# Unit 0's feed-forward by pairs of blocks, attention bundles half a step sooner, late key products further back: one kernel on one Trainium2 core

## The chip, the cores and the metric

The kernel runs on one core of a Trainium2 chip. The metric is the device time of one execution in microseconds (us), as the median of several runs. A core has five engines that run side by side, each through its own list of instructions in order: PE (TensorE, matrix products), DVE (VectorE, element by element), ACT (ScalarE, functions and copies), POOL and SP, which here issues nearly all the DMAs. PE multiplies from SBUF into PSUM, which has eight banks; DVE and ACT read PSUM and write SBUF. An instruction that waits holds up everything behind it on its engine.

## The reference, cut to what matters

```python
# q, k, v, a_re, a_im: (4, 8, 768, 48)
mag = sqrt(a_re**2 + a_im**2)
scale = minimum(mag, 0.999) / (mag + 1e-06)
a_re_n, a_im_n = a_re * scale, a_im * scale
for t in range(768):                       # S_re, S_im start at zero
    S_re, S_im = ar * S_re - ai * S_im + kv, ar * S_im + ai * S_re
    y[:, :, t] = einsum('bhd,bhde->bhe', q[:, :, t], S_re)
x = y, heads side by side                  # (3072, 384)
out = ((x @ w_a) * (x @ w_b)) @ w_out      # 384 -> 1536 -> 384
```

A linear recurrence with complex decay gives x, and a gated feed-forward net follows. All data are float32.

## The kernel before, in words

**Units.** Tokens are worked in chunks of 128 (six per sequence) and two of the four batch rows at a time. So there are 12 units: units 0 to 5 are the chunks of the first two rows, 6 to 11 those of the last two. Units 5 and 11 are the last chunks and pass no state on.

**Stages of a unit u.**
- `prep(u)` (L204 to L343) normalizes the decay, forms its running products and multiplies q and k with them. It is DVE work with some functions on ACT. Late in it: squares (ACT, L302), their sum (DVE, L308), logarithm and exponential (ACT, L309, L310), two products (DVE, L328, L330), the key product (DVE, L334) and the products of q and k (DVE, L314). The next unit's normalization, `scale` (L171), is woven in (ACT L182 to L191, DVE L183 to L197).
- `stack(u)` (L348) moves q and k from the tile qk to the tile stk by ten SBUF to SBUF DMAs on SP. There is one qk and one stk: stk is written once the attention ahead has read it, and `load_qk` (L345) of the next unit once the stacking has read qk.
- `attn(u)` (L377), for each batch row i of the two and each group of four heads: scores (PE L391) and their mask (DVE L394, the tile am), transposes of k (PE L402, copied by ACT L406), outputs (PE L431, bank x), their cast to xh (ACT L435) and the rest xl (DVE L440), and the new state (PE L447, DVE L454 and L458).
- The feed-forward of unit w works in 12 blocks of 128 columns. First products (`gemm1`, PE L498): 18 matmuls a block, on xh and xl, into banks called ab. `gated` multiplies: a copy on ACT (L502), the product h_t on DVE (L503), its cast hh on ACT (L504), the rest hl on DVE (L505). Second products (`gemm2`, PE L534): 6 matmuls a block. From unit 1 on two blocks make a pair: one bank takes a of both blocks and one b of both, so each step of `gated` works on 512 columns. The first bank is free for the next pair after L502, the second after L503.

**Start.** The weights come as 64-bit numbers and are split into two float32 parts (`split_weights`, L135) on DVE, PE and ACT, a part of it during unit 0's feed-forward. There unit 0 goes block by block (256 columns in `gated`), over three ab banks and two m banks, which scores, transposes and states share; after that there are two and three.

**Order.** While the feed-forward of unit w runs, the attention of unit w+1 is called in bundles, between the pairs. A step k counts blocks. At even k a pair's first products are called, at odd k the second products of the pair before; a bundle follows step k where k stands in `SLOTS` (L59) or, for units 5 and 11, `SLOTS_LAST`. The last bundle also ends prep(w+2) and calls its stacking, then load_qk(w+3). `drain` (L648) lets prep advance between steps by about 2400 ns of work, as its `yield`s count it. A scheduler then orders each engine's instructions by priority (the masks, casts and gated steps are raised). From w = 4 on (`LED`) PE keeps the order as written.

Of the kernel before, what the change touches and what calls it, by code (L numbers as in the profile page):

```python
# [46 lines left out]
EARLY = 2  # L47
WARM = 8
LED = 5
O_BUFS = 3  # L50
# [7 lines left out]
STACK_AT = 11  # L58
SLOTS = ((5, 7, 9, 11), (5, 7, 9, 11), (5, 7, 9, 10))  # L59
SLOTS_LAST = (6, 8, 10)  # L60

# [10 lines left out]
def tile_kernel(ctx: ExitStack, tc: tile.TileContext, a_d, qk_d, v_d, w_d, qn_d, kn_d, vn_d, an_d, out_d):  # L72
# [12 lines left out]
    ps = fast.enter_context(tc.tile_pool(name="ps", bufs=1, space=PSUM))  # L85
    turns = {"ab": [0, 1, 2], "o": [3, 4], "x": [5], "m": [6, 7]}

# [116 lines left out]
    def prep(u):  # L204
# [120 lines left out]
        if u < EARLY:  # L325
# [5 lines left out]
                                 op0=ALU.subtract, op1=ALU.mult, reverse0=True)  # L331
        yield 870
        kk = qk[:, :, 1, TOK:2 * TOK]
        vec.tensor_tensor(out=kk, in0=kk, in1=a_t[:, 0].rearrange("p (j t) -> p j t", j=NJ), op=ALU.mult)  # L334
        if rescaled(c):
# [9 lines left out]
    def load_qk(u):  # L345
        sync.dma_start(out=qk[:, :, 1, 0:2 * TOK], in_=qk_d[u])
# [30 lines left out]
    def attn(u, xh, xl):  # L377
# [82 lines left out]
        if u == 0:  # L460
            order = [(scores, 0, 0), (scores, 0, 1), (outputs, 0, 0), (outputs, 0, 1), (scores, 1, 0), (scores, 1, 1),
                     (residual, 0, 0), (outputs, 1, 0), (outputs, 1, 1), (transposes, 0, 0), (transposes, 0, 1),
                     (residual, 1, 0), (state, 0, 0), (transposes, 1, 0), (transposes, 1, 1), (state, 1, 0)]
        elif u == 1:
            order = [(scores, 0, 0), (scores, 0, 1), None, (transposes, 0, 0), (transposes, 0, 1), None,
                     (outputs, 0, 0), (outputs, 0, 1), (scores, 1, 0), (scores, 1, 1), (residual, 0, 0), None,
                     (state, 0, 0), None, (transposes, 1, 0), (transposes, 1, 1), None,
                     (outputs, 1, 0), (outputs, 1, 1), (residual, 1, 0), (state, 1, 0), None]
        elif last:
            order = [(scores, 0, 0), (scores, 0, 1), None,  # L470
                     (outputs, 0, 0), (outputs, 0, 1), (residual, 0, 0), (scores, 1, 0), (scores, 1, 1), None,
                     (outputs, 1, 0), (outputs, 1, 1), (residual, 1, 0), None]
        else:
            order = [(scores, 0, 0), (scores, 0, 1), (transposes, 0, 0), None,
                     (transposes, 0, 1), (outputs, 0, 0), (outputs, 0, 1), (residual, 0, 0), (scores, 1, 0), None,
                     (scores, 1, 1), (state, 0, 0), (transposes, 1, 0), None,
                     (transposes, 1, 1), (outputs, 1, 0), (outputs, 1, 1), (residual, 1, 0), (state, 1, 0), None]
# [205 lines left out]
    for w in range(NU):  # L683
# [6 lines left out]
        if w + 1 == LED:  # L690
            ordered.enter_context(tc.manual_schedule(engines={pe.engine}))
        if w == 0:
            for f in range(NF):
                next(ws, None)
                drain(p1, P1_F)
                if f == P1_AT:
                    drain(p1)
# [6 lines left out]
                    pgen = prep(2)  # L704
                pend.extend((w, os_, *h) for h in gemm1((f,), *x_cur))
                if len(pend) > LAG:
                    second()
                if f > STACK_AT - 6:
                    next(at, None)
            turns["ab"], turns["m"] = [0, 1], [2, 6, 7]  # L710
            drain(at)
            drain(pgen)
            stack(2)
            load_qk(3)
            pgen = prep(3)
            x_cur = x_nxt
            continue
        slots = () if last else SLOTS_LAST if (w + 1) % NCH + 1 == NCH else SLOTS[min(w, len(SLOTS)) - 1]
        for k in range(NF):
            if last and k >= NF - 2:  # L720
# [7 lines left out]
            if k in slots:  # L728
                next(at)
                if k == slots[-1]:  # L730
# [4 lines left out]
                    if w + 3 < NU:  # L735
                        load_qk(w + 3)
                        pgen = prep(w + 3)
            drain(pgen, 2400)
        x_cur = x_nxt
# [70 lines left out]
```

## Time and profile before

| | us |
|---|---|
| median of 3 runs | 694.71 (694.18 to 695.41) |
| the profiled execution, its own time | 697.03 |
| its span, first to last instruction | 694.9 |
| PE busy | 647.5 |
| DVE busy | 542.4 |
| ACT busy | 290.2 |
| granted PE clock, mean | 0.969 |

Busy times are of the whole span. The page also cuts the span into 40 slices, with each engine's busy share in tenths. A timeline row has the start in us, the duration, the engine, the line, the operation, the tiles it writes and reads, the matrix or tile sizes, a count, and in brackets how long the engine had stood idle before it and what it waited for. A row of a group has the count, busy us and mean ns, then the idle time before its instructions.

### The profile page before, as it was taken

Reading aid. Unit: us, or ns where it says so; the run is one execution under the profiler, and the core shown is the slowest. Engines: PE = TensorE matmul, PEld = TensorE weight load, DVE = VectorE, ACT = ScalarE, POOL = GpSimd, SP = SyncE. Lnnn points to the kernel's source line nnn. Section 1 sums busy time; section 2 is a strip of 40 time slices with the busy share of each in tenths; the row PEclk is TensorE's granted clock in tenths of the full one; section 3 lists DMA queues with packets and bytes.
Section 4 is the critical chain, followed back from the end, with each engine's and each line's share of the span. In section 5 each row is a group of like instructions: output and inputs, shape, how many; then the busy total and the mean of one; then the engine's idle time right before and its main releaser. Section 6 shows DMA issues by size and latency. Waiting matters only on the chain.

```text
span 694.9 us, 14053 instructions
## 1 busy us (share of the span) xinstructions
PE 647.5 (93%) x5854; PEld 609.0 (88%) x5854; DVE 542.4 (78%) x1081; ACT 290.2 (42%) x484; POOL 5.6 (1%) x11
## 2 busy tenths in 40 slices
PE   2647999999999999999899999999999989999996
PEld 1224889898999999999799999999899989999996
DVE  5999999999889999999888989989899542213211
ACT  6357665624445255362444634445241412121211
POOL 3000000000000000000000000000000000000000
PEclk9577999999999999999999999999999999999999
DMA  8973201413315133160430521430420420400000
GB/s 312 403 285 106 90 1 38 147 55 88 110 38 148 51 115 107 23 208 7 118 119 20 150 69 46 116 113 9 122 70 1 122 69 2 121 24 2 24 1 27
DMA packets 32085, 63.91 MB, mean 92 GB/s; under 512 B 3984, under 2 KB 10640, under 8 KB 32016
## 3 DMA queue, kind: packets, MB, share of 16 engines
q1 hardware_dynamic: 28560, 58.23, 27.2%
q10 hardware_dynamic: 3456, 4.72, 1.9%
q8 instruction: 48, 0.79, 0.5%
q14 instruction: 21, 0.17, 0.1%
HBM read 39.32 MB, written 4.72 MB: 63 GB/s over the span
## 4 chain that ended last, share of the span: by engine, by line
PE 55%; DVE 32%; DMA 5%; ACT 3%; issue 3%; SPq 1%; ACTq 0%; DVEq 0%
PE ab L498 28%; PE o L534 13%; PE pm L391 4%; PE xp L431 4%; DVE a_t L294 3%; PE pm L447 3%; DVE qk L314 2%; DMA w<-in_dram 2%; DVE h_t L503 2%; DVE hl L505 2%; DVE pr L231 2%; DVE z L299 2%; DVE pr L261 2%; PE pm L402 1%; DVE o_sb L143 1%
## 5 line engine op out<-in xcount | busy, mean ns | idle before, releaser
L498 PE MATMUL ab<-xh,w 128*128 128x256 f32 x1728 | 325.8, 283 | 5.0 <-ACT xh L435 2.7
L498 PEld LDWEIGHTS ab<-xh,w 128*128 128x128 f32 x1728 | 272.2, 189 | 6.8 <-ACT xh L435 3.3
L498 PE MATMUL ab<-xl,w 128*128 128x256 f32 x864 | 243.8, 282 | 1.7 <-DVE xl L440 1.7
L498 PEld LDWEIGHTS ab<-xl,w 128*128 128x128 f32 x864 | 163.8, 190 | 3.1 <-DVE xl L440 2.7
L534 PE MATMUL o<-w,hh 128*128 128x384 f32 x576 | 149.9, 340 | 0.0
L503 DVE TENSOR_TENSOR h_t<-ab,h_t 128x512 f32<-128x512 f32 (+1 forms) x79 | 50.5, 639 | 76.6 <-PE ab L498 71.5
L504 ACT CAST hh<-h_t 128x512 fp32r<-128x512 f32 (+1 forms) x79 | 45.8, 580 | 135.8 <-DVE h_t L503 135.7
L534 PEld LDWEIGHTS o<-w,hh 128*128 128x128 f32 x576 | 100.0, 188 | 0.8 <-issue 0.6
L534 PE MATMUL o<-w,hl 128*128 128x384 f32 x288 | 97.1, 337 | 0.0
L502 ACT COPY h_t<-ab 128x512 f32<-128x512 f32 (+1 forms) x79 | 42.9, 544 | 110.6 <-PE ab L498 98.5
L505 DVE TENSOR_TENSOR hl<-h_t,hh 128x512 fp32r<-128x512 f32 (+1 forms) x79 | 50.6, 641 | 12.6 <-ACT hh L504 12.4
L151 PE MATMUL ab<-o_sb,ident 128*128 128x384 f32 x42 | 27.9, 770 | 30.4 <-DVE o_sb L145 20.6
L391 PE MATMUL pm<-stk 128*128 128x128 f32 x384 | 52.9, 280 | 1.9 <-DMA stk<-qk 1.9
L534 PEld LDWEIGHTS o<-w,hl 128*128 128x128 f32 x288 | 54.0, 188 | 0.0
L391 PEld LDWEIGHTS pm<-stk 128*128 128x128 f32 x384 | 48.2, 191 | 6.1 <-issue 2.8
L231 DVE TENSOR_TENSOR pr<-z 128x384 f32<-128x384 f32 (+1 forms) x91 | 47.2, 525 | 2.8 <-ACT z L217 0.6
L294 DVE TENSOR_TENSOR a_t<-z,b_t 128x768 f32<-128x768 f32 x48 | 44.3, 953 | 0.1
L151 PEld LDWEIGHTS ab<-o_sb,ident 128*128 128x128 f32 x42 | 9.8, 277 | 39.2 <-DVE o_sb L145 29.0
L314 DVE TENSOR_TENSOR qk<-qk,z 128x768 f32<-128x768 f32 (+1 forms) x34 | 43.7, 1286 | 0.5
L431 PE MATMUL xp<-am,v_t 128*32 128x128 f32 x768 | 39.1, 276 | 0.6 <-DVE am L394 0.6
L394 DVE TENSOR_TENSOR am<-pm,mask 128x512 f32<-128x512 f32 x48 | 32.5, 684 | 3.5 <-PE pm L391 3.2
L431 PE MATMUL xp<-stk,u 128*32 128x128 f32 x640 | 32.9, 273 | 0.0
(105 smaller groups left out, 749.2 us busy)
## 6 DMA issues: line engine op xcount, KB each, us to landing
w<-in_dram SPq DMA_DIRECT2D x36, 384.0 KB, 8.1
qk<-in_dram SPq DMA_DIRECT2D x12, 768.0 KB, 4.8
a_t<-in_dram SPq DMA_DIRECT2D x11, 768.0 KB, 4.4
stk<-qk SPq DMA_DIRECT2D x42, 192.0 KB, 3.3
v_t<-in_dram SPq DMA_DIRECT2D x24, 256.0 KB, 2.7
out_dram<-o_sb ACTq DMA_DIRECT2D x24, 192.0 KB, 2.0
stk<-qk SPq DMA_DIRECT2D x18, 192.8 KB, 3.2
stk<-qk SPq DMA_DIRECT2D x14, 128.0 KB, 2.7
```

The lines of the kernel that those rows point to most:

```text
L151: pe.matmul(out=lp[:, 0:n], lhsT=ident, rhs=t, start=True, stop=False)
L231: vec.tensor_tensor(out=pr[:, :, :, o:o + n], in0=view(zz, W + at_(i) + 2 * o, [[W, 2], [-W, 2], [2, n]]), in1=tok(slice(1, 3), i - 1, o, ...
L294: vec.tensor_tensor(out=pz[:, s].rearrange("p (j b e) -> p j b e", j=SUB // 2, e=2), in0=zb[:, 1 + s], in1=view(bb, (1 + k - s) * NB, [[0, ...
L314: vec.tensor_tensor(out=qk4[:, :, k, x0:x1], in0=qk4[:, :, 1, x0:x1], in1=z[:, k].rearrange("p (j t) -> p j t", j=NJ).unsqueeze(2).broadca ...
L391: pe.matmul(out=sp[:, h4], lhsT=stk[:, h, ks], rhs=stk[:, h, qs], start=True, stop=True)
L431: pe.matmul(out=xp[qd * 32:(qd + 1) * 32, ti], lhsT=l, rhs=rr, start=st, stop=sp_, tile_position=(0, qd * 32), skip_group_check=True)
L498: pe.matmul(out=ab, lhsT=r(w_ab(f, part, m * NJ + i)), rhs=r(xt[:, i, :]), start=n == 0, stop=n == 8)
L502: act.copy(out=h_t, in_=a)
L503: vec.tensor_tensor(out=h_t, in0=b, in1=h_t, op=ALU.mult)
L504: act.copy(out=r(hh), in_=h_t)
L505: vec.tensor_tensor(out=r(hl), in0=h_t, in1=hh, op=ALU.subtract)
L534: pe.matmul(out=os_[tt][:, 0:DM], lhsT=r(ht[:, ts]), rhs=r(w_t[f, 2][:, part, :]), start=(f == 0 and n == 0), stop=(f == NF - 1 and n == 2))
```

## The change

Four things are changed. Unit 0's feed-forward runs by pairs like the others, and with two ab and three m banks from the start. Unit 1's attention is called in the four bundles that units 2 to 10 have, at steps 5, 7, 9 and 11, where there were six. From w = 4 on (attention from unit 5) the bundles come half a step sooner: 4, 6, 8, 9 for 5, 7, 9, 10, and 5, 7, 9 for 6, 8, 10 with units 5 and 11. For units 6 and up `prep` yields 9000 before the key product, so that its call falls into the next step, and the scheduler is told to leave that product where it was called.

```diff
+LATE = 6
-SLOTS = ((5, 7, 9, 11), (5, 7, 9, 11), (5, 7, 9, 10))
-SLOTS_LAST = (6, 8, 10)
+SLOTS = ((5, 7, 9, 11), (5, 7, 9, 11), (5, 7, 9, 11), (5, 7, 9, 10), (4, 6, 8, 9))
+SLOTS_LAST = (5, 7, 9)
-    turns = {"ab": [0, 1, 2], "o": [3, 4], "x": [5], "m": [6, 7]}
+    turns = {"ab": [0, 1], "o": [3, 4], "x": [5], "m": [2, 6, 7]}
...
         yield 870
+        if u >= LATE:
+            yield 9000
         kk = qk[:, :, 1, TOK:2 * TOK]
-        vec.tensor_tensor(out=kk, in0=kk, in1=a_t[:, 0].rearrange("p (j t) -> p j t", j=NJ), op=ALU.mult)
+        keys = vec.tensor_tensor(out=kk, in0=kk, in1=a_t[:, 0].rearrange("p (j t) -> p j t", j=NJ), op=ALU.mult)
+        if u >= LATE:
+            tc.keep_in_program_order(keys)
...
-        elif u == 1:
-            order = [(scores, 0, 0), (scores, 0, 1), None, (transposes, 0, 0), (transposes, 0, 1), None,
...
-        if w == 0:
-            for f in range(NF):
+        slots = () if last else SLOTS_LAST if (w + 1) % NCH + 1 == NCH else SLOTS[min(w, len(SLOTS) - 1)]
+        for k in range(NF):
+            if w == 0:
                 next(ws, None)
                 drain(p1, P1_F)
-                if f == P1_AT:
+                if k == P1_AT:
...
-                pend.extend((w, os_, *h) for h in gemm1((f,), *x_cur))
-                if len(pend) > LAG:
-                    second()
-                if f > STACK_AT - 6:
-                    next(at, None)
-            turns["ab"], turns["m"] = [0, 1], [2, 6, 7]
-            drain(at)
-            drain(pgen)
-            stack(2)
-            load_qk(3)
-            pgen = prep(3)
-            x_cur = x_nxt
-            continue
-        slots = () if last else SLOTS_LAST if (w + 1) % NCH + 1 == NCH else SLOTS[min(w, len(SLOTS)) - 1]
-        for k in range(NF):
...
-            drain(pgen, 2400)
+            if w > 0:
+                drain(pgen, 2400)
```

After the change the line numbers from L49 on are higher by one, at the key product (L334) by three, from L335 to L463 by five; from L469 to L691 they are the same as before. Three places in the engines' order follow. First ACT around unit 5's attention, during unit 4's feed-forward. xh is the cast of the outputs; z, chk and sc belong to prep(7) and the normalization woven into it. Before:

```order
L310 ACTIVATE a_t<-a_t,biases 128x768
L502 COPY h_t<-ab 128x512
L504 CAST hh<-h_t 128x512
L435 CAST xh<-xp 128x3x128
L502 COPY h_t<-ab 128x512
L217 ACTIVATE z<-z 128x768
L182 ACTIVATE a_t,chk<-a_t 128x1536
L504 CAST hh<-h_t 128x512
L184 ACTIVATE sc<-a_t,biases 128x768
L435 CAST xh<-xp 128x3x128
```

After (L440 is the cast, L183 and L185 are L182 and L184 before):

```order
L303 ACTIVATE a_t<-z 128x1536
L440 CAST xh<-xp 128x3x128
L310 ACTIVATE a_t<-a_t,biases 128x768
L311 ACTIVATE a_t<-a_t,biases 128x768
L502 COPY h_t<-ab 128x512
L504 CAST hh<-h_t 128x512
L440 CAST xh<-xp 128x3x128
L218 ACTIVATE z<-z 128x768
L183 ACTIVATE a_t,chk<-a_t 128x1536
L502 COPY h_t<-ab 128x512
L185 ACTIVATE sc<-a_t,biases 128x768
```

Both casts have moved ahead; the second now stands before the normalization's square and logarithm instead of behind them.

Second, DVE around unit 11's key product, from the state of unit 9 (u) on. Before:

```order
L454 TENSOR_TENSOR u_105<-pm,u_105 96x4x2x48
L458 TENSOR_TENSOR u_105<-u_105,stk 96x4x2x48
L503 TENSOR_TENSOR h_t<-ab,h_t 128x512
L505 TENSOR_TENSOR hl<-h_t,hh 128x512
L334 TENSOR_TENSOR qk<-qk,a_t 128x3x256
L314 TENSOR_TENSOR qk<-qk,z 128x3x512
L503 TENSOR_TENSOR h_t<-ab,h_t 128x512
```

After, from the product of L330 before on (L337 is the key product, L399 a mask of unit 10, L315 the products of q and k):

```order
L331 SCALAR_TENSOR_TENSOR a_t<-a_t 128x768
L503 TENSOR_TENSOR h_t<-ab,h_t 128x512
L505 TENSOR_TENSOR hl<-h_t,hh 128x512
L503 TENSOR_TENSOR h_t<-ab,h_t 128x512
L505 TENSOR_TENSOR hl<-h_t,hh 128x512
L503 TENSOR_TENSOR h_t<-ab,h_t 128x512
L505 TENSOR_TENSOR hl<-h_t,hh 128x512
L503 TENSOR_TENSOR h_t<-ab,h_t 128x512
L399 TENSOR_TENSOR am<-pm,mask 128x512
L505 TENSOR_TENSOR hl<-h_t,hh 128x512
L399 TENSOR_TENSOR am<-pm,mask 128x512
L337 TENSOR_TENSOR qk<-qk,a_t 128x3x256
```

Four pairs' h_t and hl and two masks stand ahead of the key product, where there was one pair.

Third, DVE in prep(6), between the sum of squares and the product that waits for ACT's logarithm and exponential. Before:

```order
L299 TENSOR_TENSOR z<-a_t 128x768
L505 TENSOR_TENSOR hl<-h_t,hh 128x512
L394 TENSOR_TENSOR am<-pm,mask 128x512
L308 TENSOR_TENSOR a_t<-a_t 128x768
L328 TENSOR_TENSOR a_t<-a_t 128x768
```

After (L300, L309 and L329 are L299, L308 and L328 before):

```order
L300 TENSOR_TENSOR z<-a_t 128x768
L505 TENSOR_TENSOR hl<-h_t,hh 128x512
L309 TENSOR_TENSOR a_t<-a_t 128x768
L445 TENSOR_TENSOR xl<-xp,xh 128x3x128
L399 TENSOR_TENSOR am<-pm,mask 128x512 x2
L329 TENSOR_TENSOR a_t<-a_t 128x768
```

Between the sum and the product that waits, where nothing stood, stand now a rest xl and two masks. In prep(8) two masks and an hl have moved into the same place, in the others little has.

More of the change, by code (lines that the diff above doesn't have):

```diff
@@ L463, in attn @@
                      (residual, 1, 0), (state, 0, 0), (transposes, 1, 0), (transposes, 1, 1), (state, 1, 0)]
-        elif u == 1:
-            order = [(scores, 0, 0), (scores, 0, 1), None, (transposes, 0, 0), (transposes, 0, 1), None,
-                     (outputs, 0, 0), (outputs, 0, 1), (scores, 1, 0), (scores, 1, 1), (residual, 0, 0), None,
-                     (state, 0, 0), None, (transposes, 1, 0), (transposes, 1, 1), None,
-                     (outputs, 1, 0), (outputs, 1, 1), (residual, 1, 0), (state, 1, 0), None]
         elif last:
```

## The prediction

> **What bounds the kernel now.** I read the slices first, then the engines' busy time by stage, then each place at which TensorE (PE) stands still.
>
> ```profile
> PE   2647999999999999999899999999999989999996
> DVE  5999999999889999999888989989899542213211
> PEclk9577999999999999999999999999999999999999
> ...
> 80.00:172.60 92.60, 90.79 (x738) 83.42 (x736) 88.44 (x194) 49.70 (x93) 0.00 (x0) 1.00 0.21 62
> 344.00:545.00 201.00, 197.13 (x1897) 193.26 (x1895) 182.35 (x355) 87.51 (x137) 0.00 (x0) 0.99 0.26 77
> 568.00:694.90 126.90, 121.08 (x1124) 119.14 (x1123) 31.38 (x50) 26.43 (x48) 0.00 (x0) 0.98 0.10 28
> ```
>
> A windows row holds the stretch, its length and then the busy time of PE, weight loads, VectorE (DVE) and ScalarE (ACT). After about 75 us PE is full. DVE is nearly as full until 545 us (88.44 of 92.60 us, 182.35 of 201.00), and after 568 us it has a quarter of that load. So a PE stop that goes is time won only as far as DVE can follow. The timeline of PE (weight loads are PEld) shows its stops, with what ended each in brackets:
>
> ```profile
> 172.59 0.49 PE L391 MATMUL pm<-stk 128*128 128x128 f32 x2 [1.68 <-DMA stk<-qk]
> ...
> 347.13 0.19 PEld L498 LDWEIGHTS ab<-xh,w 128*128 128x128 f32 x1 [2.71 <-ACT xh L435]
> 347.73 0.29 PEld L498 LDWEIGHTS ab<-xl,w 128*128 128x128 f32 x1 [0.41 <-DVE xl L440]
> ...
> 498.98 0.19 PEld L498 LDWEIGHTS ab<-xl,w 128*128 128x128 f32 x1 [1.48 <-DVE xl L440]
> ...
> 565.94 0.23 PEld L498 LDWEIGHTS ab<-xh,w 128*128 128x128 f32 x1 [2.46 <-DVE h_t L503]
> ```
>
> Two of them cost more than the stop, as the chain of work that ended last shows (start, us, what), and the granted clock (third number from the end) behind them:
>
> ```profile
> 347.73 5.84 PE ab L498 x35
> ...
> 355.69 4.23 PE ab L498 x36
> ...
> 565.94 3.92 PE ab L498 x18
> ...
> 347.10:353.60 6.50, 6.25 (x38) 6.06 (x39) 5.29 (x12) 4.77 (x6) 0.00 (x0) 0.74 0.57 153
> 565.90:569.90 4.00, 3.96 (x20) 3.96 (x21) 2.25 (x2) 1.20 (x2) 0.00 (x0) 0.57 0.00 0
> ```
>
> A pair's 36 first products take 4.23 us. After the stop at 344 us, 35 took 5.84, so 1.7 us more than their 4.1; after the one at 563 us, 18 took 3.92 instead of 2.1, so 1.8 more. The clock fell to 0.74 and 0.57 there. The Trainium skill (TensorE: Matmul & The Clock Gate, section Why this matters for your kernels) says that idle gaps above about 3 us bring the half clock back. By that rule gaps of 2.7 and 2.5 us would have no such tail, and the sum below would be 3.5 us smaller; these two rows show the tail, and the measurement decides.
>
> **The change part by part.** The sum is made against the profiled execution: span 694.9 us within 697.03, so 2.1 us lie around it. The median of the runs shown, 694.71, is 2.3 us below that execution; I take the same gain off the median.
>
> (1) Unit 0 by pairs. Each DVE row of 256 columns pairs up into one of 512:
>
> ```profile
> L505 DVE TENSOR_TENSOR hl<-h_t,hh 128x512 fp32r<-128x512 f32 x65 | 44.7, 688 | 12.0 <-ACT hh L504 11.9
> L503 DVE TENSOR_TENSOR h_t<-ab,h_t 128x512 f32<-128x512 f32 x65 | 44.5, 685 | 71.7 <-PE ab L498 71.5
> L503 DVE TENSOR_TENSOR h_t<-ab,h_t 128x256 f32<-128x256 f32 x14 | 5.9, 423 | 4.9 <-ACT h_t L502 4.9
> L505 DVE TENSOR_TENSOR hl<-h_t,hh 128x256 fp32r<-128x256 f32 x14 | 5.9, 422 | 0.6 <-ACT hh L504 0.5
> ```
>
> 12 x (423 + 422) - 6 x (685 + 688) = 1.90 us of DVE, all of it ahead of unit 2's last products, whose transfer PE awaits at 172.59. DVE is busy 96% of that stage, so I let the 1.9 pass through; PE stood 1.68 there, and its own work to that point is the same, so I take **1.7 us**. Bounds: a first pair gives DVE its first product 18 matmuls later (18 x 4.23 / 36 = 2.1 us); if DVE idles for that, the part is -0.2. If PE too comes sooner, it is 1.9.
>
> Taken at nothing here: the third bank that ab loses. In the conversion of weights PE waits for DVE's splitting, so a later bank hides behind it:
>
> ```profile
> PE ab L151 <- DVE o_sb L145: 20.6, 13, 6.3
> ```
>
> Without that cover each of the 21 conversions on ab could wait for one ACT copy; I keep 1 us as the end. Unit 1's attention in four bundles has the same matmuls; fewer products stand between its scores and outputs, so PE may wait for two mask products (0.7 us each), bounds 0 to 1.4, taken at 0.
>
> (2) The last bundle of unit 5 (and 11) goes ahead of a pair's first products. The stop at 344 us came thus:
>
> ```profile
> 342.06 0.40 PE L431 MATMUL xp<-stk,u 128*32 128x128 f32 x8
> ...
> 344.79 0.95 DVE L183 SCALAR_TENSOR_TENSOR a_t<-a_t 128x768 f32<-128x768 f32 x1
> ...
> 345.78 0.94 ACT L184 ACTIVATE sc<-a_t,biases 128x768 f32<-128x768 f32 x1 [0.71 <-DVE a_t L183]
> ...
> 346.62 0.46 ACT L435 CAST xh<-xp 128x384 fp32r<-128x384 f32 x1
> ```
>
> Outputs ended at 342.4; the cast of xh stood in ACT's queue behind the logarithm L184, which waited for DVE. From outputs to the next unit's first product there were only 2.1 us of second products; now a pair's first products (4.2) come between: 6.3 us, against the 5.3 that xl took (342.4 to 347.7, where PE gets it). And in the new order the cast stands ahead of the logarithm. Won: 2.71 + 0.41 of stop and 1.7 of slow clock, **4.8 us**. Late next: nothing until the first h_t of unit 5, part (5).
>
> (3) The fourth bundle of units 6 to 10 likewise. The stop at 497.5 us waited for xl behind four products on DVE; with 4.2 us more ahead of it, its 1.48 goes: **1.5 us**. Half a step sooner also frees stk sooner, and SP issues the next unit's stacking sooner; the DMA share there is 0.26, so I cost the collision at 0.
>
> (4) Unit 11's key products.
>
> ```profile
> 554.94 0.61 SPq L346 DMA_DIRECT2D qk<-in_dram  x1
> ...
> 562.53 0.96 DVE L334 TENSOR_TENSOR qk<-qk,a_t 128x768 f32<-128x768 f32 x1 [7.24 <-DMA out_dram<-o_sb]
> ...
> 565.20 0.68 DVE L503 TENSOR_TENSOR h_t<-ab,h_t 128x512 f32<-128x512 f32 x1
> ...
> qk<-in_dram SPq DMA_DIRECT2D x1, 768.0 KB, 7.2
> ```
>
> L334 stood at DVE's head for 7.24 us. The output's DMA is named, but qk's load, issued at 554.94 and 7.2 us under way, lands at that moment and is what L334 reads. L503, which frees PE's bank, was queued behind it. Now three more pairs' h_t and hl and two masks stand ahead of L334, about 3 x 6.35 us later (a pair is 4.23 + 2.1), far behind the landing. Won: 2.46 + 1.8 = **4.3 us**. For units 6 to 10 the products move by a mask or two; the stacking that follows them has cover:
>
> ```profile
> 468.30 1.67 DVE qk L314
> ...
> 492.73 6.97 SPq L358 DMA_DIRECT2D stk<-qk  x10
> ```
>
> Unit 9's products began at 468.3, yet its stacking waited until 492.7 for the attention ahead to leave stk: over 20 us in which a later product costs nothing. SP's loads of a_t and v_t queue between the two, under the same cover.
>
> (5) Given back to DVE.
>
> ```profile
> 491.38 0.19 PEld L498 LDWEIGHTS ab<-xh,w 128*128 128x128 f32 x1
> ...
> 495.44 0.68 DVE L503 TENSOR_TENSOR h_t<-ab,h_t 128x512 f32<-128x512 f32 x1
> ...
> L503 DVE TENSOR_TENSOR h_t<-ab,h_t 128x512 f32<-128x512 f32 x24 | 16.4, 683 | 1.0 <-PE ab L498 1.0
> ...
> L328 DVE TENSOR_TENSOR a_t<-a_t 128x768 f32<-128x768 f32 x5 | 4.8, 958 | 6.7 <-ACT a_t L310 6.7
> L308 DVE TENSOR_TENSOR a_t<-a_t 128x768 f32<-128x768 f32 x5 | 4.8, 955 | 5.0 <-ACT a_t L302 5.0
> ```
>
> From 344 to 545 us DVE waited for PE's h_t input 1.0 us in all: it was behind, by 3.9 us at 491.5. PE bears about 4.2 (second products 2.1 and half of the next pair's first, until it needs the bank). So the 6.3 us of (2) and (3) must also come out of DVE's waits: that 1.0, and the 11.7 for ACT. The new order puts two masks into such a wait for units 6 and 8, by 1.4 us each (two masks), and little for the others; I take 3.3 in all. That leaves 6.3 - 1.0 - 3.3 = **2.0 us** lost again in small stops. Ends: 0 (the queue may grow) and 5.3 (no wait is filled).
>
> Sum: 1.7 + 4.8 + 1.5 + 4.3 - 2.0 = 10.3 us; 694.71 - 10.3 = **684.4 us**.
>
> **The rivals.** A: DVE is the bound until 545 us and fills none of its waits: 5.3 come back instead of 2.0, 7.0 won, 687.7 us. For it: DVE's 182 of 201 us. Against: the waits that the new order fills.
>
> B: the key products, 4.5 us with their two L314, now hold DVE in unit 9's step and PE stops there instead, so (4) is not won and that part does not do what it says: 6.0 won, 688.7 us. For it: the next pair's h_t stands right behind them. Against: DVE has spare time after 545 us, and PE bears 4.2.
>
> C, the other side: the third and fourth bundles now have only the second products between them.
>
> ```profile
> 484.79 1.05 PE L391 MATMUL pm<-stk 128*128 128x128 f32 x8
> ...
> 486.99 0.51 PE L402 MATMUL pm<-ident,stk 96*128 96x96 f32 x4
> ...
> 488.82 0.68 DVE L394 TENSOR_TENSOR am<-pm,mask 128x512 f32<-128x512 f32 x1
> ```
>
> The fourth bundle's transposes need the bank that this mask frees. The mask was done 3.7 us after the scores (485.84 to 489.50). The way from scores to transposes was 1.7 us of state and transposes and 4.2 of first products; it is now 1.7 + 2.1 = 3.8. For it: 3.7 against 3.8. If DVE is later by d, five units (6 to 10) pay d each: at d = 1 us, 5.3 won, 689.4. From d = 2.1 on (10.3 / 5) the kernel is slower, and stops near 2.5 us drew the slow clock (1.75 us): 5 x 4.25 - 10.3 = 11 us slower, 705.7 us. Against: in the new order only one h_t stands directly ahead of this mask.
>
> **How the numbers follow.** Forecast 0.60 (own range 681.5 to 687). A 0.17, B 0.08, C at 1 us 0.05, C slower 0.07, C near break-even 0.03. The range 680.8 to 689.5 holds the forecast's unknowns (the 2.0 at 0 and PE sooner at unit 0 below) and A, B and the mild C. Runs differ by about 0.2%, 1.4 us, so that is what counts as the same. So faster 0.90 (0.60 + 0.17 + 0.08 + 0.05), same 0.03, slower 0.07.
>
> **What would show it.** The stops at 344, 497 and 563 us should be gone from PE, with both low clocks (all slices from 80 us at 9); L334 of unit 11 without a wait; scores of unit 2 near 171 us with under 0.5 us of stop; 12 fewer DVE rows by L503 and L505. Part (5) shows as new stops of under 1 us for DVE's h_t, xl or masks between 340 and 545 us, 2 us in all; over 5 means A. Stops at the fourth bundle's transposes mean C. I am wrong if a stop over 2.5 us appears anywhere new.

## The result, and the profile after

The kernel after takes 689.87 us (median of 14 executions, 688.52 to 693.54) against 693.80 us for the kernel before, executed beside it (692.18 to 697.36). The ratio is **0.9937**, with a 95% interval of 0.9921 to 0.9953: faster by 4.4 us, where 10.3 were forecast. (The two medians lie 3.9 us apart. Gains in us below are worked out from the ratios.) The profiled execution of after took 688.80 us (span 687.1), 8.2 us less than the profiled one of before, which took 697.03: the one lies 1.1 us below its median, the other 3.2 above. The distance between the two profiles is thus about twice the distance between the medians, and that is the question of the experiments.

The slices of after, and its stages in the form that the prediction used (length, then busy time of PE, weight loads, DVE and ACT, the granted clock third from the end):

```profile
PE   3647999999999999999999899999999999999996
...
DVE  6999999999989999999998989989989644223221
...
PEclk9577999999999999999999999999999999999999
...
80.00:172.60 92.60, 90.61 (x735) 83.55 (x734) 87.92 (x181) 48.51 (x81) 0.00 (x0) 1.00 0.21 62
344.00:545.00 201.00, 197.72 (x1913) 193.72 (x1912) 183.25 (x355) 86.88 (x136) 0.00 (x0) 1.00 0.28 81
545.00:568.00 23.00, 23.00 (x182) 23.00 (x181) 8.96 (x12) 5.08 (x9) 0.00 (x0) 1.00 0.19 64
```

The stops at 344, 497 and 563 us are gone, and so are the low clocks behind the first and the last: from 545 to 568 us PE is busy without a gap, at clock 1.00. What stands still now is this (PE's timeline, with what ended each stop in brackets):

```profile
170.94 0.49 PE L396 MATMUL pm<-stk 128*128 128x128 f32 x2 [1.45 <-DMA stk<-qk]
...
383.19 0.55 PE L407 MATMUL pm<-ident,stk 96*128 96x96 f32 x4 [1.31 <-DVE am L399]
...
534.72 0.55 PE L407 MATMUL pm<-ident,stk 96*128 96x96 f32 x4 [1.12 <-DVE am L399]
```

Unit 2's scores still wait for the stacking, though they come 1.65 us sooner (170.94 for 172.59). And the transposes of the fourth bundle of units 6 and 9 wait for the third's mask. DVE's timeline shows why at unit 6:

```profile
380.98 0.96 DVE L216 TENSOR_TENSOR z<-a_t,sc 128x768 f32<-128x768 f32 x1
381.86 0.68 DVE L503 TENSOR_TENSOR h_t<-ab,h_t 128x512 f32<-128x512 f32 x1
382.46 0.68 DVE L399 TENSOR_TENSOR am<-pm,mask 128x512 f32<-128x512 f32 x1
```

The mask stood behind a product of prep and an h_t. This is the mechanism of rival C, in two of the five units. From 344 to 545 us PE stands 3.3 us in all (201.00 less 197.72).

To compare executions, I take from PE's rows when each unit's first products start and when those of its seventh block do (its middle). The steps in between, in us, for four profiles of the kernel before and four of the kernel after (the later ones come from the experiments below):

```text
                        before                        after
                        1st   2nd   3rd   4th         1st   2nd   3rd   4th
unit 0 to its middle    28.94 28.96 28.92 28.93       25.48 25.53 25.53 25.51
middle of 0 to unit 1   40.94 40.94 40.95 40.91       40.10 40.01 40.06 42.08
middle of 1 to unit 2   34.01 33.76 33.66 33.87       33.48 33.83 33.74 35.88
unit 4 to unit 5        48.45 48.23 48.21 48.45       46.19 46.04 46.03 46.01
unit 5 to its middle    23.15 23.20 21.70 23.23       21.25 21.19 21.21 21.24
middle of 5 to unit 6   27.26 27.32 27.64 27.29       28.94 29.13 28.98 29.15
middle of 8 to unit 9   28.81 28.81 28.81 28.81       30.01 30.03 30.18 30.13
unit 9 to its middle    25.11 24.71 21.30 23.10       21.15 21.20 21.15 21.20
whole span              694.9 694.7 691.0 693.5       687.1 687.2 687.0 692.8
```

Executions of one kernel do not agree: unit 9's first half takes 21.3 to 25.1 us before, and after the change unit 0's and unit 1's second halves each have two lengths, 2 us apart. The long one of unit 1 is no mark of the change: two kernels of the experiments that leave units 0 to 3 as before (e3 and e11) show it too, with 35.8 and 35.6 us.

### The profile page after: what moved, and what is told of

It reads as the page before. It is cut to its first block, busy times and chain, and to the rows that moved or that the text cites. A ratio compares the mean times of both kernels' runs of the same rounds, so it can differ in the third digit from the quotient of the medians.

```text
span 687.1 us, 14031 instructions
## 1 busy us (share of the span) xinstructions
PE 643.3 (94%) x5854; PEld 605.4 (88%) x5854; DVE 542.3 (79%) x1069; ACT 288.8 (42%) x472; POOL 5.6 (1%) x11
## 4 chain that ended last, share of the span: by engine, by line
PE 48%; DVE 34%; DMA 7%; ACT 5%; issue 4%; SPq 1%; DVEq 0%; ACTq 0%
PE ab L498 26%; PE o L534 12%; DMA w<-in_dram 5%; PE pm L396 4%; DVE a_t L295 4%; PE xp L436 3%; DVE qk L315 3%; DVE h_t L503 2%; PE pm L452 2%; DVE hl L505 2%; DVE pr L232 2%; DVE z L300 2%; DMA stk<-qk 2%; DVE pr L262 2%; DVE am L399 2%
## 5 line engine op out<-in xcount | busy, mean ns | idle before, releaser
L498 PE MATMUL ab<-xh,w 128*128 128x256 f32 x1728 | 322.5, 281 | 0.1
L503 DVE TENSOR_TENSOR h_t<-ab,h_t 128x512 f32<-128x512 f32 (+1 forms) x73 | 49.5, 678 | 73.9 <-PE ab L498 69.4
L505 DVE TENSOR_TENSOR hl<-h_t,hh 128x512 fp32r<-128x512 f32 (+1 forms) x73 | 49.6, 680 | 13.6 <-ACT hh L504 13.5
L315 DVE TENSOR_TENSOR qk<-qk,z 128x768 f32<-128x768 f32 (+1 forms) x34 | 43.6, 1284 | 0.6
L399 DVE TENSOR_TENSOR am<-pm,mask 128x512 f32<-128x512 f32 x48 | 32.1, 683 | 2.3 <-PE pm L396 2.0
```

The lines of the kernel that those rows point to most:

```text
L315: vec.tensor_tensor(out=qk4[:, :, k, x0:x1], in0=qk4[:, :, 1, x0:x1], in1=z[:, k].rearrange("p (j t) -> p j t", j=NJ).unsqueeze(2).broadca ...
L399: vec.tensor_tensor(out=am, in0=sp, in1=mask[:].unsqueeze(1).broadcast_to([128, 4, 128]), op=ALU.mult)
L498: pe.matmul(out=ab, lhsT=r(w_ab(f, part, m * NJ + i)), rhs=r(xt[:, i, :]), start=n == 0, stop=n == 8)
L503: vec.tensor_tensor(out=h_t, in0=b, in1=h_t, op=ALU.mult)
L505: vec.tensor_tensor(out=r(hl), in0=h_t, in1=hh, op=ALU.subtract)
```

## The experiments

The first theory (S) was that the profile of before showed an unusual execution; its rivals were that the parts win what was forecast but do not add up, or that single parts win nothing. Four kernels were timed side by side: the kernel before again, and each part of the change alone.

**e1, the kernel before again** (no edit).

> The kernel before, unchanged, once more with a profile. The profiled executions of before and after lie 8.2 us apart (697.03 and 688.80), the medians 3.9 (693.80 and 689.87); so either the first profile showed a slow execution, or it showed the usual one and the gain was given back where the profile of after doesn't show it. Theory S (the sizes were read from an unusual execution): the profiled time lies near 693.8 us, and of the 3.5 us of slow clock behind the stops at 344 and 563 us, and of the stops themselves (2.71 and 2.46 us), at least 3 us are missing in this execution. Theory N (the sizes are usual, the parts don't add up): both stops within 0.4 us of those sizes, with the granted clock under 0.8 behind them, whatever the time. Ratio 1.000 within 0.002 by both.

Measured: 695.96 us, ratio 1.0006 (0.9989 to 1.0024); its profiled execution took 696.87 us. The stops were there again, 2.24 + 0.21 us at 347 us and 1.82 us at 565 us, with the slow clock behind both:

```profile
347.80:354.00 6.20, 6.20 (x39) 6.20 (x40) 4.83 (x11) 4.00 (x5) 0.00 (x0) 0.72 0.56 143
565.50:569.50 4.00, 4.00 (x21) 4.00 (x22) 2.80 (x3) 1.19 (x2) 0.00 (x0) 0.64 0.00 0
```

By this one profile theory S falls. It came back later in another form, as theory T.

**e2, unit 0's pairs, the banks and unit 1's bundles alone** (on the kernel after):

```diff
-LATE = 6
+LATE = 99
-SLOTS = ((5, 7, 9, 11), (5, 7, 9, 11), (5, 7, 9, 11), (5, 7, 9, 10), (4, 6, 8, 9))
-SLOTS_LAST = (5, 7, 9)
+SLOTS = ((5, 7, 9, 11), (5, 7, 9, 11), (5, 7, 9, 11), (5, 7, 9, 10))
+SLOTS_LAST = (6, 8, 10)
```

> Unit 0 by pairs, the banks and unit 1's four bundles alone; bundles from unit 5 on and the key product as before. The prediction's term (1) is 1.7 us: 692.1 us, ratio 0.9975. Theory S: 0.9975 to 0.999, since the stop at 172.6 us (1.68 us) shrinks little (1.61 us in the profile of after) while PE comes there about 1.5 us sooner. Theory N: the same 0.9975 alone, and it is lost again by the end of unit 2 when the others are added. Rival P (the pairs win nothing, since the first pair gives DVE its product 2.1 us later): 1.000 or above.

**e3, the sooner bundles alone** (on the kernel before):

```diff
-SLOTS = ((5, 7, 9, 11), (5, 7, 9, 11), (5, 7, 9, 10))
-SLOTS_LAST = (6, 8, 10)
+SLOTS = ((5, 7, 9, 11), (5, 7, 9, 11), (5, 7, 9, 10), (4, 6, 8, 9))
+SLOTS_LAST = (5, 7, 9)
```

> The bundles of units 5 to 11 half a step sooner alone, on the kernel before. The prediction's terms (2), (3) and (5) give 4.8 + 1.5 - 2.0 = 4.3 us: 689.5 us, ratio 0.9938. Theory S: about half, 1.5 to 3 us, 0.9957 to 0.998, with the stop at 344 us gone from the profile. Theory N: 4.3 us alone, of which the other parts take some away. Rival C (stops at the fourth bundle's transposes, of which the profile of after has two, 1.47 and 1.28 us): stops of over 1 us at two or more of these places, and no gain, 0.999 or above.

**e4, the later key product alone** (on the kernel before):

```diff
+LATE = 6
...
+        if u >= LATE:
+            yield 9000
...
+        if u >= LATE:
+            tc.keep_in_program_order(keys)
```

> Only the later key product (the yield of 9000 and the kept order, units 6 to 11), on the kernel before. The prediction's term (4) is 4.3 us: 689.5 us, ratio 0.9938. Theory S: 1.5 to 3 us, 0.9957 to 0.998, with the stop at 563 us gone. Theory N: 4.3 us alone. Rival K (the later product holds up the stacking of units 6 to 10 as much as it wins at unit 11): 0.999 or above, with a stop in front of the scores of one of these units.

Measured: pairs 0.9977 (0.9958 to 0.9997), sooner 0.9969 (0.9954 to 0.9983), late 0.9953 (0.9936 to 0.9970): 1.6, 2.2 and 3.3 us of 695.13 (the medians lie 1.2, 2.3 and 4.4 us below it). By the ratios each is below its term or at it, and their sum, 7.1, is above what the whole wins. The profiles show one reason: **the stop near 563 us is gone in all three.** With the sooner bundles and with the pairs, too, unit 9's first half takes 21.2 us (with the pairs a stop of 1.0 us near 546 us came in its place, for ACT's copy of the transposes, with a slow clock behind it: the step to unit 9 takes 31.5 us there, not 28.8). The sooner bundles have the two stops at the fourth bundle that after has, near 386 and 538 us, so rival C is true of them, but they still win. With the later product alone the stop at 347 us was there (2.23 + 0.21 us), and no slow clock followed it (1.00 from 347.8 to 354 us); the stop at 497 us was gone.

Next, the whole with one part taken out, beside the whole.

**e5, the kernel after again** (no edit).

> The kernel after, unchanged, beside the three that follow. Alone the parts won 1.6 (pairs), 2.2 (sooner) and 3.3 us (late), 7.1 in sum; all together won 4.4. Theory O (overlap: the stop at 563 us, 2.4 us and its slow clock, is lost by each part alone, as their profiles show, and so is counted up to three times): ratio 0.993 to 0.9955 again. Theory A (the parts add up, and the first comparison of the whole was low): 0.990. Theory T (after a stop of about 1.5 to 2.5 us the slow clock follows in some executions and not in others): the 1.6 us stop before unit 2's scores is there again; the clock behind it is 1.00 or near 0.72, not between.

**e6, after without the later key product:**

```diff
-LATE = 6
+LATE = 99
```

> The kernel after with the key product called as before (no yield of 9000, no kept order): pairs and sooner bundles stay. Theory O: the stop at 563 us stays away, since sooner bundles alone removed it; within 0.7 us of the whole change, ratio 0.9935 to 0.996. Theory A: the 3.3 us of the later product are missing, 0.9965 to 0.998, with a stop of 2 us or more near 560 us.

**e7, after without the pairs** (the kernel before with the sooner bundles and the `LATE` lines).

> The kernel before with the sooner bundles and the later key product: the whole change without unit 0's pairs, the banks and unit 1's bundles. Its distance to the whole change is what the pairs bring there. Prediction's term (1): 1.7 us, so ratio 0.9955 to 0.9965 if the whole is at 0.9935. Theory O: the gain of the pairs alone (1.6 us) came from the stop at 563 us, whose 4 us were gone there in exchange for 2.7 us near 545 us; beside the others the pairs then bring what the profile shows at the end of unit 1, 1.5 to 2 us, less what the stop before unit 2's scores takes back, 0.5 to 2 us in all.

Measured: the whole 689.99 us, 0.9920 (0.9892 to 0.9949); without the later product 689.39 us, 0.9915 (0.9886 to 0.9944); without the pairs 692.98 us, 0.9949 (0.9927 to 0.9970). The whole lies between what theories O and A expected; the version without the later product, 0.6 us from it, speaks for O. So beside the sooner bundles the later key product, good for 3.3 us alone, wins nothing that shows, and the pairs some 2 to 3. The timeline of after without the later product shows the overlap (SP's issue of qk's load, and the key product on DVE; the rows of before, at 554.94 and 562.53 us, stand in part (4) of the prediction):

```profile
552.01 0.61 SPq L351 DMA_DIRECT2D qk<-in_dram  x1
...
557.26 0.96 DVE L337 TENSOR_TENSOR qk<-qk,a_t 128x768 f32<-128x768 f32 x1 [1.89 <-DMA qk<-in_dram]
```

Unit 9's first product started at 548.72 and at 550.18 us. The load was issued 6.2 us behind it before, and 1.8 us behind it here: the fourth bundle of unit 9 goes half a step sooner, stk comes free sooner, the stacking and then the load follow. The key product then starts 7.1 us behind unit 9's first product instead of 13.8. Over the kernels in which it was not moved, with the length of unit 9's first half beside it:

```text
key product starts behind unit 9's first product, us    first half of unit 9, us
before, 1st profile          13.8                        25.1
before, 2nd                  13.4                        24.7
before, 4th                  13.3                        23.1
before, 3rd                  11.5                        21.3
units 9, 10 put back (e13)   11.5                        21.3
extra matmuls (e11)          11.2                        21.1
pairs alone                   8.8                        21.2
after without late            7.1                        21.2
sooner alone                  6.5                        21.2
```

Up to 11.5 us PE does not notice; from 13.3 on it stops.

**e8, the fourth bundle of units 6 to 10 at step 10** (on the kernel after; second and first products between third and fourth):

```diff
-(5, 7, 9, 10), (4, 6, 8, 9))
+(5, 7, 9, 10), (4, 6, 8, 10))
```

> The kernel after with the fourth bundle of units 6 to 10 at step 10 instead of 9, so that second and first products (6.3 us) lie between the third and the fourth; the third stays at 8. Rival C of the prediction (transposes of the fourth bundle wait for the third's mask; 1.47 and 0.63 us near 382 us, 1.28 us near 533 us, 3.4 us in all in the profile of after): these stops go, and the stops at the fourth bundle's outputs that were there before (1.4 us at 497 us) come back in one or two units: 0 to 2 us faster than the whole change, ratio 0.9905 to 0.994. Against C (those stops only stand in for DVE's lateness, which comes out elsewhere): the same as the whole change within 0.5 us, or slower.

Measured: 689.92 us, 0.9915 (0.9890 to 0.9940), the same as the whole beside it. The stops near 382 and 533 us went (unit 9 starts 28.66 us behind the middle of unit 8, not 30.0), but unit 6's second state stopped for 2.2 us instead, with a slow clock behind it.

**e9, units 6 to 10 back at their old steps** (on the kernel after; units 5 and 11, the pairs and the later product stay):

```diff
-(5, 7, 9, 10), (4, 6, 8, 9))
+(5, 7, 9, 10))
```

> The kernel after with units 6 to 10 at their old steps 5, 7, 9, 10; units 5 and 11 sooner, the later key product and the pairs stay. In the profiles, the sooner bundles of units 6 to 10 cost 1.2 to 1.6 us in unit 6's step (28.9 us from the middle of unit 5 to unit 6, 27.3 before) and 1.2 us in unit 9's (30.0 against 28.8), and the 1.4 us stop at 497 us, which they should remove, was gone with the later key product alone. Theory C (term (3) of the prediction is a loss): 2.0 to 2.8 us faster than the whole change, span near 685 us, ratio to the kernel before 0.988 to 0.991. Against it (the prediction's term (3) is a gain of 1.5): 1.5 us slower than the whole, 0.994 to 0.996, with the stop at 497 us back.

Measured: 692.16 us, 0.9945 (0.9926 to 0.9964). Neither expectation held as a whole. The steps of units 7 to 9 are as short as theory C said (28.81 us to unit 9, no stop at 497 us), but unit 6 has a new stop (ACT's timeline, then PE's):

```profile
390.37 0.94 ACT L187 ACTIVATE sc<-sc,biases 128x768 f32<-128x768 f32 x1
391.33 0.84 ACT L188 ACTIVATE sc<-sc 128x768 f32<-128x768 f32 x1
392.08 0.46 ACT L411 COPY kt<-pm 128x384 f32<-128x384 f32 x1
...
392.60 0.62 PE L452 MATMUL pm<-v_t,kt 128*96 128x48 f32 x5 [2.44 <-ACT kt L411]
```

The copy of the transposes stands in ACT's list behind four functions of the normalization, and with a slow clock behind the stop the step to unit 6 takes 30.9 us.

**e10 and e12, two more profiles of the kernel before**, and **e11, extra matmuls in the stop at 344 us**:

> The kernel before, a third profile. Theory T (the slow clock follows a stop of 1.5 to 2.6 us in some executions only): of the three places with such a stop (before unit 2's scores near 172 us, 1.7 to 1.8; near 347 us, 2.9; near 565 us, 2.0 to 2.5), at least one has another clock than in the two profiles so far (1.00, then below 0.8 twice), and the time differs from 697 us by about 1.7 us for each. Theory N (it follows from the length of the stop): the same clocks and 697 us within 0.5.

> The kernel before, a fourth profile; as for the third: theory T expects the clocks behind the stops near 172, 347 and 565 us to differ between the four profiles, theory N expects 1.00, 0.79 and 0.81 each time.

```diff
+FILL = 20
...
+            for _ in range(fill):
+                pe.matmul(out=ab[0][:, 0:TOK], lhsT=r(w_ab(0, 0, 0)), rhs=r(w_t[0, 2][:, 0, 0:TOK]), start=True, stop=True)
...
-                pend.extend((w, os_, *h) for h in gemm1((k, k + 1), *x_cur))
+                pend.extend((w, os_, *h) for h in gemm1((k, k + 1), *x_cur, fill=FILL if w == 5 and k == 0 else 0))
```

> The kernel before with 20 extra matmuls of 256 columns (2.4 us, their product is overwritten) ahead of unit 5's first products, so that PE stands for 0.7 us at 344 us where it stood 2.9. The products themselves start no sooner, so only the slow clock behind the stop can be won. Theory N (1.7 us of slow clock in every execution, as the prediction took it): ratio 0.9975. Theory T (in some executions only): 0.998 to 0.9995, and the profile shows clock 1.00 from 347 to 354 us.

Measured: the two single executions took 693.08 and 695.55 us. Third, then fourth profile, behind the stops at 347 and 565 us:

```profile
347.80:354.00 6.20, 5.65 (x42) 5.45 (x43) 5.96 (x13) 5.08 (x7) 0.00 (x0) 1.00 0.62 172
565.50:569.50 4.00, 4.00 (x31) 4.00 (x30) 2.16 (x4) 1.21 (x2) 0.00 (x0) 1.00 0.00 0
```

```profile
347.80:354.00 6.20, 5.99 (x36) 5.79 (x37) 5.14 (x11) 4.65 (x6) 0.00 (x0) 0.72 0.54 148
565.50:569.50 4.00, 3.46 (x25) 3.46 (x26) 3.29 (x4) 1.21 (x2) 0.00 (x0) 1.00 0.00 0
```

In the third the stop at 348 us was there (2.22 + 0.22 us) and no slow clock followed; the stop near 563 us was not there at all, since qk's load was issued 0.5 us sooner behind unit 9's first product and took 1.8 us less. In the fourth the slow clock followed the first stop and not the second (1.72 us). Theory T holds: the same kernel's executions differ by these (what decides stands in the last section). How long that load was under way in the third profile, by the groups of DMA issues from 545 us on (KB each, median us), where the first had 7.2:

```profile
qk<-in_dram SPq DMA_DIRECT2D x1, 768.0 KB, 5.4
```

The kernel with the extra matmuls took 694.01 us, 0.9982 (0.9961 to 1.0002), with clock 1.00 behind 347 us; its interval holds both expectations, so it decides nothing.

**e13, units 9 and 10 put back, no later product** (on e6's kernel):

```diff
-(5, 7, 9, 10), (4, 6, 8, 9))
+(5, 7, 9, 10), *((4, 6, 8, 9),) * 4, (5, 7, 9, 10))
```

> The kernel after without the later key product (as in e6) and with units 9 and 10 at their old steps 5, 7, 9, 10; units 6 to 8 stay at 4, 6, 8, 9. Theory O (the sooner fourth bundle of unit 9 lets SP issue the load of qk for unit 11 about 4.4 us sooner, and that alone removes the stop near 563 us): the load is issued about 6.2 us behind unit 9's first product again (1.8 in e6, 6.2 before), the key product waits at the head of DVE's list, the stop of 0 to 2.5 us is back, unit 9's first half takes 21.3 to 25.1 us (21.2 in e6), and the time is 0 to 3 us above e6's once 1.2 us at unit 9's fourth bundle are won back: ratio 0.992 to 0.996. Against O: no stop, load still issued within 3 us.

Measured: 691.25 us, 0.9947 (0.9920 to 0.9973); the kernel after, timed beside it (e16), 690.81. The load was issued 5.8 us behind unit 9's first product (1.8 in e6), so it is unit 9's bundle that moves it (unit 10's is called only later). The stop did not return in the profiled execution: the load took about as long as in the third profile of before, 5.75 us from its issue to the key product, which started 11.5 us behind unit 9's first product. How often the stop comes without the later product and with the old steps was not measured apart.

**e14, unit 6 at the sooner steps, units 7 to 10 at the old ones**, **e15, unit 6 later still**, and e16, after once more (on the kernel after):

```diff
-(5, 7, 9, 10), (4, 6, 8, 9))
+(5, 7, 9, 10), (4, 6, 8, 9), (4, 6, 8, 9), (5, 7, 9, 10))
```

> The kernel after with units 7 to 10 at their old steps 5, 7, 9, 10; unit 6 stays at 4, 6, 8, 9, units 5 and 11 at 5, 7, 9, and the later key product stays. Theory C (beside the later key product the sooner bundles of units 7 to 10 cost 0.5 us in unit 6, 0.5 in unit 8's first half and 1.2 in unit 9, as the steps of the profiles of after and of the later key product alone show): 2 us below the whole change, span near 685 us where no slow clock falls in, ratio 0.988 to 0.9905. Prediction's term (3): 1.5 us slower than the whole.

```diff
-(5, 7, 9, 10), (4, 6, 8, 9))
+(5, 7, 9, 10), (5, 7, 9, 11), (5, 7, 9, 11), (5, 7, 9, 10))
```

> As e14, with unit 6 at 5, 7, 9, 11. In e9 (5, 7, 9, 10) its second state waited 2.6 us for the copy of k's transposes, which stood in ACT's list behind four functions of the normalization, with 1.7 us of slow clock behind it. If one more half pair puts that copy ahead of them or far behind, the stop is under 0.7 us, unit 6's step (middle of unit 5 to unit 6) 27.3 us as before against 28.9, and the time 1.6 us below e14's: ratio 0.986 to 0.9885. If the copy still stands behind them: a stop of 2 us or more there, as slow as e9, 0.9925 to 0.996.

> The kernel after, unchanged, on the same chip as the three others. So far 0.9937 (0.9921 to 0.9953) and 0.9920 (0.9892 to 0.9949). Theory O and T together: 0.992 to 0.995 again, with stops of 1.6 to 2.1 us before unit 2's scores, 1.5 near 382 us and 1.3 near 533 us in the profile.

Measured: 688.83 us, 0.9911 (0.9879 to 0.9944); 692.88 us, 0.9973 (0.9953 to 0.9993); after 690.81 us, 0.9942 (0.9919 to 0.9965). The later steps for unit 6 stopped its second state for 1.7 us and the first products behind it for 0.8 and 0.7 us, slower than either expectation. The first kernel looked better than after, so both ran again as e17 and e18.

> e14's kernel again, beside the kernel after. Theory C: 1.5 to 2.5 us below the kernel after's median on this chip, ratio to the kernel before 0.989 to 0.9915; unit 9's first products start 28.8 us after the middle of unit 8, against 30.0. Against it (e14's 7 executions were lucky): within 0.7 us of the kernel after.

> The kernel after, unchanged, beside e17. Its comparisons so far gave 0.9937, 0.9920 and 0.9942; by the overlap of the parts 0.992 to 0.995 again. By the sum of the prediction 0.985.

Measured: **687.49 us, 0.9893** (0.9862 to 0.9923) against 691.54 us, 0.9943 (0.9922 to 0.9964) for after. The version with the sooner steps for units 5, 6 and 11 alone beats the kernel before, and its median lay below after's both times, by 2.0 and 4.1 us. Its steps at units 7 to 9 are 2.1 us shorter in sum than after's (28.81 for 29.18, 21.11 for 21.63 and 28.81 for 30.01); the rest of the 4.1 us between these two medians is in no step that this edit touches, and may lie in what executions differ by.

The profiled execution of the kernel after in the last run was a long one, 694.51 us, and shows what after's first profile had not (ACT's timeline, then PE):

```profile
129.56 1.48 ACT L183 ACTIVATE a_t<-a_t 128x1536 f32<-128x1536 f32 x1 [3.07 <-DMA a_t<-in_dram]
...
131.04 0.85 ACT L154 ACTIVATE w<-pm 128x384 fp32r<-128x384 f32 x2
...
131.57 2.10 PE L396 MATMUL pm<-stk 128*128 128x128 f32 x16 [1.48 <-ACT w L154]
```

```profile
126.64 1.49 ACT L183 ACTIVATE a_t<-a_t 128x1536 f32<-128x1536 f32 x1 [1.05 <-DMA a_t<-in_dram]
...
128.13 0.85 ACT L154 ACTIVATE w<-pm 128x384 fp32r<-128x384 f32 x2
...
129.03 1.89 PE L396 MATMUL pm<-stk 128*128 128x128 f32 x14
```

The first piece is this execution, the second after's first profile. Unit 1's scores waited for ACT's copy of a converted weight (L154), which reads a bank of the kind that the scores write; the copy stood in ACT's list behind the square of a normalization (L183), and that waited for the load of the decay into a_t. Of twelve profiles of kernels with the pairs, five have this stop, and in each the scores start within 0.1 us of the end of the first of the two copies. The load took 5.8 to 6.6 us in these five and 4.7 to 5.0 in the other seven; the second half of unit 0 takes 41.7 to 42.3 us in the five, and 39.9 to 40.2 in the others. The eight profiles without the pairs do not have the stop: there the load took 4.2 to 4.6 us. Behind unit 2's scores the clock fell too (0.87 from 171 to 177 us, 1.00 in after's first three profiles).

## Why the prediction was wrong

**The direction held, and the stops named went; two steps of the sum failed.** The stops at 344, 497 and 563 us are gone, both low clocks too, 12 DVE rows of L503 and L505 are fewer, and unit 11's key product waits no more.

**The step that failed first is "I take the same gain off the median".** The sum was made of one execution, 3.2 us above its median; it held both slow clocks and qk's load at its longest. Terms (2) and (4) took all of it as won. The four profiles of before say what a usual one holds: against after's 21.2 us, unit 5's first half lost 1.9, 2.0, 0.5 and 2.0 us, mean 1.6; unit 9's lost 3.9, 3.5, 0.1 and 1.9, mean 2.4. Together 4.0, where the first profile has 5.9. And the kernel after has accidents too: its first profile was free of them, its fourth, with the stop before unit 1's scores and a slow clock behind unit 2's, is 5.7 us longer. The means of four spans, 693.5 and 688.5, lie 5.0 us apart, as the four timed comparisons do (0.9937, 0.9920, 0.9942, 0.9943: 4 to 5.6 us); the first profiles lie 7.8 apart. What after's long executions hold was seen in few of them; that it makes up the rest of the distance is worked out from eight profiles, not measured apart.

**The second is term (3) and what was given back in (5).** Forecast 1.5 won and 2.0 lost. Between the first profiles of the two kernels unit 8's first half won 0.8 (22.42 to 21.63), and unit 6's step lost 1.7, unit 7's 0.6 and unit 9's 1.2. That is 2.7 lost where 0.5 was forecast. Rival C priced d = 1 us in five units; it came at 1.1 to 1.3 us in two, with small ones beside it, and at unit 6 with a stop of 0.5 us for the copy of the transposes too. The stop at 497 us that term (3) was to win goes with the later key product alone: unit 8's first half takes 21.1 us there (e4), 22.4 before. The version that leaves units 7 to 10 alone has steps 2.1 us shorter there, so this part of the change is a loss.

Point by point:

- (1) Unit 2's scores came 1.65 us sooner for 1.7 forecast, but that agreement is luck, a sum of terms that were mis-sized. The third bank that ab loses was costed at nothing; unit 0's first products start at 77.8 us in the mean of twelve profiles with the pairs and at 75.7 in eight without (76.3 to 78.9 against 74.8 to 77.0). So 2.0 us are lost there, by the bank or by the order of the pairs; no run separates the two. The pairs then win 3.4 us in unit 0's first half (28.9 to 25.5) and 0.9 in the second, where the stop before unit 1's scores does not come; unit 1's first half loses 1.1 (18.1 to 19.1). That PE would reach unit 2's scores no sooner was wrong: it got there 1.4 us sooner too, and still stands for 1.45 us.
- (2) 4.2 us by the first profiles (48.45 to 46.19 and 23.15 to 21.25) for 4.8. The 2.71 + 0.41 us that the term took are gaps between weight loads; between PE's products the rows of the same place show 2.39 + 0.21, half a us less.
- (4) 4.0 us by the first profiles for 4.3 (the gap between products was 2.25 us, that between weight loads 2.46). But **the cause named is only one of two**: the later key product alone removes the stop (e4), and the sooner bundle, which issues the load 4.4 us sooner, removes it as well, so the later product adds nothing that shows beside it (e6). The prediction had seen that SP issues the stacking sooner and costed that at 0; it did not follow it to the load that term (4) waits for. So it booked as the work of one edit what either does. The whole's time did not suffer from that; what each part is worth did.
- Rival B did not come about: the key products held nothing up in unit 9. Rival A, by which DVE gives back 5.3 us in small stops, did not either: PE stands 3.3 us in all from 344 to 545 us, and most of that at masks, where C has it.
- The range was too narrow because it had no term for how executions of one kernel differ, 692 to 701 us for before.

The Trainium skill's rule (TensorE: Matmul & The Clock Gate, section Why this matters for your kernels) that gaps above about 3 us bring the slow clock back was set aside on two rows. Rows of more executions agree with neither reading: the gap near 347 us, 2.2 to 2.4 us, was followed by it in three of four profiles of before, and gaps of 1.7 to 1.8 us at times.

## What to carry to other kernels

Before a stop and its slow clock go into a sum, look at the same stop in several executions, and take the mean; a gain between two profiles says little until it stands beside the spread of either kernel. Where two edits touch the same chain (a bundle that frees a tile, the transfer into it, the product that reads it), follow the sooner release to its end, or one stop is won twice in the sum. When a block of work is moved sooner, ask of each unit by itself whether the engine that answers it has the time: here the move paid at unit 5; at unit 6, with unit 5 moved, it cost less than the old steps (29.2 us for its step, not 30.9); at unit 11 it changed nothing (45.8 us from the first products of unit 10 to those of 11, before and after); and it cost in units 7 to 9.

## What the runs showed of the hardware

The slow clock behind a PE stop is not a matter of its length alone: it matters where the stop falls. In each of the twenty profiles the granted clock is 1.00 or 0.50, and the times at which it changes lie whole multiples of 3.41 us apart. So it follows a grid, and where that grid lies differs from execution to execution. Cut along the grid, the stops at 344 and 563 us of before's first profile, and the first of them in its third (345.9 to 348.1 us), look like this (length of the stretch, then PE's busy time; the granted clock third from the end):

```profile
344.16:347.58 3.42, 0.96 (x5) 0.44 (x3) 3.39 (x7) 2.63 (x6) 0.00 (x0) 1.00 0.79 201
347.58:350.99 3.41, 3.26 (x15) 3.26 (x16) 3.20 (x9) 2.87 (x4) 0.00 (x0) 0.50 0.78 203
562.62:566.03 3.41, 1.16 (x11) 0.95 (x9) 3.38 (x4) 0.11 (x1) 0.00 (x0) 1.00 0.00 0
566.03:569.44 3.41, 3.41 (x16) 3.41 (x17) 2.12 (x2) 1.09 (x2) 0.00 (x0) 0.50 0.00 0
```

```profile
343.77:347.18 3.41, 2.15 (x12) 1.82 (x11) 3.29 (x6) 2.60 (x4) 0.00 (x0) 1.00 0.76 187
347.18:350.60 3.42, 2.25 (x16) 2.05 (x17) 3.25 (x9) 3.36 (x5) 0.00 (x0) 1.00 0.75 202
350.60:354.01 3.41, 3.41 (x28) 3.41 (x27) 3.31 (x7) 2.34 (x4) 0.00 (x0) 1.00 0.53 141
```

In the first profile each stop lies within one stretch, and the next one has half the clock. In the third a border of the grid cuts a stop of about the same size in two, and the clock stays. From 80 to 682 us in the twenty profiles, PE stood still for 1.79 us or more of a full-clock stretch 13 times, and half the clock followed each time; for 1.70 to 1.79 us 8 times, and it followed 3 times; after less it followed once, behind 1.04 us (pairs alone, near 546 us), and why is open. A half-clock stretch costs about half its length, 1.7 us by this estimate. So a stop of PE of 1.8 to 2.6 us draws it or not by chance.

How long a load of 768 KB takes is the other thing that differs. Issued 5.7 to 6.2 us behind unit 9's first product, qk's took 5.4 to 7.2 us in the four profiles of before, and whether PE stops near 563 us went with it. Issued 1.1 to 2.0 us behind, in the four profiles of after, it took 4.8 to 4.9.
